# LayerNorm's scaling and split on ScalarE and VectorE, one cast for q and k, and another order for the first weights

## The chip, the cores and the metric

The kernel runs on one core of one Trainium2 chip. The metric is the time of one execution on the device, in microseconds (us); lower is better. The engines are named as the profile names them: PE (TensorE, matmuls and transposes), PEld (its weight loads), DVE (VectorE), ACT (ScalarE), POOL (GpSimd) and SP (SyncE, which issues the DMAs here). Each engine works through its own queue in the order in which the instructions were put there.

## What is computed

Eight batches, each with eight heads of block-causal attention over 576 positions, whose outputs are joined to 512 columns and go through a gated feed-forward part:

```python
# q, k, v: (8, 8, 576, 64); blocks of 64 positions
scores = (q @ k.T) / 8;  masked where block(i) < block(j)
attn   = softmax(scores)                   # sum + 1e-9 below
x      = attn @ v                          # joined over heads: (8, 576, 512)
h      = gelu(x @ w_in)                    # w_in: (512, 1024), tanh form
u, v   = h[..., :512], h[..., 512:]
v_n    = (v - mean(v)) / sqrt(var(v) + 1e-6) * g_ln
v_s    = w_sg @ v_n + b_sg                 # over positions, w_sg: (576, 576)
out    = x + (u * v_s) @ w_out             # w_out: (512, 512)
```

`w_in` and `w_out` arrive as float64 and are turned into float32 on the chip, from their words. Products with full precision are made of three products of a shorter float32 form: a value x is split into hi (x cast to that form) and lo (x minus hi), and hi*hi, hi*lo and lo*hi are added.

## The kernel before, in words

The unit of work is a pair of heads: 32 pairs (`PAIRS`), four for each batch. `slot(n, sc)` (line 724) does one pair: it finishes pair n (transposes of the probabilities, products with v, normalising) and makes the scores and exponents of pair n+1 in between. Four slots make a batch; with n counted from 0, the slots n % 4 = 0, 1, 2, 3 are called A, B, C and D here.

The feed-forward part of a batch is a generator in four parts that yield after every bank of results: `v_part` (5 pieces), `u_part` (8), `s_part` (8, the spatial product with w_sg) and `o_part` (8). After each D slot the parts of that batch are put on a list (line 821): v, u, the o of the batch before, then s. `hole(k)` (line 703) runs the next k pieces. Each slot has seven holes, and `PLAN` (line 720) says how many pieces each takes: all get one, the last of D two. `FIRST` (line 722) is the plan of the slots 4 to 7, in which there is no o yet: 21 pieces in 28 holes. So in the steady state A does v and two pieces of u, B six of u and one of o, C seven of o, and D eight of s.

Only PE keeps the order in which the program is written (`PIN`, line 58: `mm` and `turn` pin each matmul behind the instruction traced before it on PE). For DVE, ACT, POOL and SP the framework simulates the program with estimated durations and puts an instruction into the queue when its inputs and its buffer are there by that estimate; the written order is the priority among those that are ready. `paced` (line 522) pins a single instruction behind the one traced before it on its engine.

The LayerNorm of a batch is a list of small steps, `side`, that `run_side(k)` takes k at a time between the holes: GELU on ACT, `moments` (line 572, DVE), `inverse_std` (line 586, POOL), `centre` (line 579, DVE) and `scale` (line 590). `scale` handles one tile of 128 rows by 512: POOL multiplies by the inverse deviation in place, DVE casts the result to hi, POOL subtracts for lo. `s_part` begins by running all that is left of `side` (lines 645 to 647), and `need("s")` (line 644) runs the weight steps that are still missing.

Weights come in 30 steps (`weights`, line 274): 8 for v's half of w_in, 1 for the gains, 4 and 4 for u's half, 5 for w_sg, 8 for w_out. A step of w_in or w_out (`load_weight`, line 219) has a DMA of 256 KB, four parts ahead, one ACT and three DVE instructions that make float32 of float64 (`from_f64`, line 199; tiles `raw` and `w`), a cast on ACT and a subtraction on POOL. Four steps stand in the prologue (lines 805 to 813), and `load_share` (line 714) spreads `WS` (line 712) over the slots: 2, 2, 2, 2, 4, 3, 4, 4, 3.

`split_qk(n)` (line 125) casts q and k of a pair on DVE, one after the other, and subtracts on POOL; it stands in slot n-2. `va.split` (line 497) does the same for x, the attention's output; it is put off to the end of the next slot (`pending`, lines 774 to 793), except in D, where the one put off and D's own run at once. x is also stored to DRAM (`spill`), and `o_part` loads it again (tile `xr`, line 681) when it begins a column block, adds the result and stores it to `out_T` (line 697). x and xr share three buffers (`KINDS`, line 65). The inverse sums of the softmax are `inverse` (line 438).

Of the kernel before, what the change touches and what calls it, by code (L numbers as in the profile page):

```python
# [9 lines left out]
F32 = mybir.dt.float32  # L10
# [18 lines left out]
def kernel(  # L29
# [49 lines left out]
    def pbank(name):  # L79
        return bank("p", name, 3)  # L80

    def pin(ins, e):
        return tc.keep_in_program_order(ins) if e in PIN else ins

    def mm(*a, **k):
        return pin(nc.tensor.matmul(*a, **k), "P")  # L86
# [26 lines left out]
    def load_qk(n):  # L113
        b, h = PAIRS[n]
        if n == 0:

            q_f, k_f = page(F32, S, "w"), page(F32, S, "w")
        else:
            q_f = sp.tile([P, S], F32, tag="q_f", name="q_f", bufs=1)
            k_f = sp.tile([P, S], F32, tag="k_f", name="k_f", bufs=1)  # L120
        SP.dma_start(q_f, qT[b, h : h + 2].rearrange("a d s -> (a d) s"))
        SP.dma_start(k_f, kT[b, h : h + 2].rearrange("a d s -> (a d) s"))
        qk[n] = (q_f, k_f)

    def split_qk(n):
        q_f, k_f = qk[n]
        parts = []
        for x, name in ((q_f, "q"), (k_f, "k")):
            hi = sp.tile([P, S], F32R, tag=name + "_h", name=name + "_h")
            V.tensor_copy(hi, x)  # L130
            parts.append(hi)
        for x, name, hi in ((k_f, "k", parts[1]), (q_f, "q", parts[0])):
            lo = sp.tile([P, S], F32R, tag=name + "_l", name=name + "_l", bufs=1)
            G.tensor_tensor(lo, x, hi.bitcast(F32), op=ALU.subtract)
            parts.append(lo)
        q_h, k_h, k_l, q_l = parts
        qk[n] = [(q_h, k_h), (q_h, k_l), (q_l, k_h)]

    def load_v(n):
# [20 lines left out]
    mask = cp.tile([P, MW], BF16, name="mask")  # L160
    G.memset(mask, 0.0)
    G.memset(mask[:BLK, MW - BLK :], -8.0e9)
    half = cp.tile([P, NT], F32, name="half")
    G.memset(half, -0.5)
    stats = cp.tile([P, NT, 2], F32, name="stats")
# [33 lines left out]
    def from_f64(raw, dh, dl):  # L199

        n = raw.shape[-1]
        words = raw.bitcast(U32).rearrange("p (n t) -> p n t", t=2)
        hi, lo = words[:, :, 1], words[:, :, 0]
        tm = page(U32, 2 * n, "w")
        t, m = tm[:, :n], tm[:, n:]


        A.activation(m.bitcast(F32), hi.bitcast(F32), AF.Abs, scale=2.0**-112)

        V.tensor_scalar(t, lo, 29, None, op0=ALU.logical_shift_right)  # L210
# [79 lines left out]
    def need(part):  # L290

        while any(p == part for p, _ in weights):
            weight_step()
# [90 lines left out]
    class Values:  # L384
# [53 lines left out]
        def inverse(self):  # L438

            r = sp.tile([P, NT * 2], F32, tag="ri", name="ri", bufs=2)  # L440
            V.tensor_scalar_add(r, self.sm.rearrange("p i a -> p (i a)"), 1e-9)
            V.reciprocal(r, r)
            self.rx = sp.tile([P, NT, 2 * D], F32, tag="rx", name="rx", bufs=1)
            G.tensor_copy(
                self.rx.rearrange("p i (a d) -> p (i a) d", a=2),
                r.unsqueeze(2).broadcast_to([P, NT * 2, D]),
            )
# [63 lines left out]
    def run_side(k):  # L511

        while k > 0 and side and side[0][0] != "G":
            k -= 1
            side.popleft()[1]()
# [4 lines left out]
            side.popleft()[1]()  # L520

    def paced(ins, e):
        return ins if e in PIN else tc.keep_in_program_order(ins)

    def gelu(tiles, after):

# [8 lines left out]
    def accumulator(name):  # L535
        return sbank(name)

    def feed_forward(b):
# [4 lines left out]
        parts = (b, vv, vn, vn_t, u, g_s)  # L543
        return v_part(*parts), u_part(*parts), s_part(*parts), o_part(*parts)

    def v_part(b, vv, vn, vn_t, u, g_s):
        need("v")
        x_s = xs[b]
        for st in (NT - 1, *range(NT - 1)):
# [40 lines left out]
        def scale(st):  # L590
            x = vv[st]
            rows = x.shape[0]
            r = rs[:rows, st : st + 1]
            paced(G.tensor_tensor(x, x, r.broadcast_to([rows, DH]), op=ALU.mult), "G")
            if st < NT - 1:
                hi, lo = vn[st] = page(F32R, DH, "vh"), page(F32R, DH, "vl")
                V.tensor_copy(hi, x)
                G.tensor_tensor(lo, x, hi.bitcast(F32), op=ALU.subtract)
            else:
                V.tensor_copy(vone[:TAIL, :], x)  # L600
                V.tensor_copy(vn_t[:TAIL, :], x)
                V.tensor_tensor(
                    vn_t[BLK:, :], x, vn_t[:TAIL, :].bitcast(F32), op=ALU.subtract
                )

        side.append(("G", lambda: gelu(vv, last)))
        for st in range(NT):
# [4 lines left out]
        for st in (NT - 1, *range(NT - 1)):  # L612
            side.append(("V", lambda st=st: scale(st)))

    def u_part(b, vv, vn, vn_t, u, g_s):
        x_s = xs.pop(b)
        for fo in range(NC):
            need(f"u{fo}")
            u.append(page(F32, S, "u"))
            fs = slice(fo * P, (fo + 1) * P)  # L620
            for th in (0, 1):
# [18 lines left out]
                    side.append(("G", lambda: gelu(u, last)))  # L640
                yield "u"

    def s_part(b, vv, vn, vn_t, u, g_s):
        need("s")
        for _ in (0, 1):
            run_gelu()
            run_side(len(side))
        for dt in range(NC):
            ghi, glo = page(F32R, S, "gh"), page(F32R, S, "gl")
            g_s.append((ghi, glo))  # L650
            for th in (0, 1):
# [22 lines left out]
    def o_part(b, vv, vn, vn_t, u, g_s):  # L674
        need("o")
        x_r = {}
        for mo, th in [(mo, th) for mo in range(NC) for th in (0, 1)]:
            ts = slice(th * SH, (th + 1) * SH)
            if th == 0:
                x_r[mo] = page(F32, S, "xr")  # L680
                SP.dma_start(x_r[mo], spill.pop((b, mo)))
            x = x_r[mo]
            acc = accumulator("acco")
            ms = slice(mo * P, (mo + 1) * P)
# [24 lines left out]
            except StopIteration:  # L709
                work.popleft()  # L710

    WS = [2, 2, 2, 2, 4, 3, 4, 4, 3]

    def load_share(n, k):

# [3 lines left out]

    PLAN = ["1111111", "1111111", "1111111", "1111112"]  # L720

    FIRST = ["1111111", "1111111", "1010101", "1010010"]

    def slot(n, sc):
        va = Values(n, sc)
# [45 lines left out]
            nx.exponents(2)  # L771
        hole(g[4])
        va.normalise()
        last = n % (H // 2) == H // 2 - 1
        if last:
            for f in pending:
                f()
            pending.clear()
            va.split()
        run_side(2)  # L780
        if n + 2 < N:
            split_qk(n + 2)
# [3 lines left out]
        run_side(3)  # L786
        hole(g[6])
        run_side(3)
        for f in pending:
            f()  # L790
        pending.clear()
        if not last:
            pending.append(va.split)
        return nx

    pending = []
# [73 lines left out]
```

## Time and profile before

| | |
|---|---|
| median of 3 runs | 837.57 us (836.84 to 838.59) |
| the profiled execution | 838.82 us, its span 836.9 us |
| PE busy | 788.5 us, 94% of the span, 5926 instructions |
| DVE busy | 531.6 us, 64%, 1504 instructions |
| ACT busy | 424.4 us, 51%, 1124 instructions |
| POOL busy | 352.7 us, 42%, 402 instructions |
| HBM read and written | 45.78 MB and 18.87 MB |

The span goes from the first instruction to the end of the last one; the time of an execution holds some 2 us more. Rows of the profile name a line, an engine, an operation and its tiles as out<-in; line L99 and L86 are helpers through which nearly all instructions go, so tiles tell the groups apart. In a row of the timeline stand start, duration, engine, line, operation, tiles, shape and count, and in square brackets how long the engine had been idle and who ended that. PE's busy time counts matmuls whose ends are modelled, so a matmul that waits inside the pipeline can look busy. PEclk is the granted clock of TensorE as a share of full speed.

### The profile page before, as it was taken

The numbers are of one execution on the slowest core, as the hardware profiler recorded it, in microseconds if no ns is written. First come the engines' busy times: TensorE is split into PE (matmuls) and PEld (weight loads), VectorE is DVE, ScalarE is ACT, GpSimd is POOL, SyncE is SP. The second block draws the span as 40 slices with busy tenths as digits, with TensorE's granted clock in tenths as the row PEclk, the third lists the DMA queues.
The fourth block names the chain that finished last, engine by engine and source line by source line (L and its number), as shares of the span: only waits on it lengthen the run. The fifth ranks groups of instructions, "written<-read, shape, count | busy, mean of one in ns | idle before, by whom it ended". The sixth has DMA issues, their size and how long they took to land.

```text
span 836.9 us, 15898 instructions
## 1 busy us (share of the span) xinstructions
PE 788.5 (94%) x5926; PEld 649.0 (78%) x5926; DVE 531.6 (64%) x1504; ACT 424.4 (51%) x1124; POOL 352.7 (42%) x402
## 2 busy tenths in 40 slices
PE   5798992999999999999999999999999999999998
PEld 3466871878878888887887878788787878878998
DVE  6876474894865658564776747766586647753432
ACT  4776663656654367344653357642764446531400
POOL 5445158461543417432372513634164323713251
PEclk8799995999999999999999999999999999999999
DMA  7233205221122112310133101321123201230031
GB/s 251 77 114 115 85 18 159 80 61 57 44 86 99 58 58 72 126 59 30 58 108 120 58 28 31 126 101 57 58 71 122 77 16 57 75 112 29 1 114 71
DMA packets 46912, 65.67 MB, mean 78 GB/s; under 512 B 4082, under 2 KB 22514, under 8 KB 46836
## 3 DMA queue, kind: packets, MB, share of 16 engines
q1 hardware_dynamic: 46836, 64.67, 24.1%
q8 instruction: 46, 0.75, 0.4%
q14 instruction: 30, 0.25, 0.1%
HBM read 45.78 MB, written 18.87 MB: 77 GB/s over the span
## 4 chain that ended last, share of the span: by engine, by line
PE 63%; DVE 20%; ACT 6%; DMA 5%; POOL 3%; issue 3%; SPq 0%; DVEq 0%; ACTq 0%; POOLq 0%
PE accs L86 14%; PE accv L86 13%; PE acco L86 9%; PE ob L86 9%; PE s L86 7%; PE pb L89 3%; DVE prob L99 3%; DVE bs L99 3%; DVE vh L99 2%; DVE vv L99 2%; PE pa L89 2%; PE accu L86 2%; ACT prob L99 2%; PE pc L89 2%; DMA xr<-spill 2%
## 5 line engine op out<-in xcount | busy, mean ns | idle before, releaser
L99 ACT ACTIVATE prob<-prob,negm 128x448 f32<-128x448 f32 (+3 forms) x320 | 178.0, 558 | 157.8 <-DVE negm L99 154.1
L99 DVE CUSTOM_DVE_ANT_0 prob<-s,mask 128x288 f32<-128x288 f32 (+2 forms) x320 | 119.4, 421 | 37.2 <-PE s L86 36.5
L99 POOL TENSOR_TENSOR q_l<-q_f,q_h 128x576 fp32r<-128x576 f32 x31 | 44.2, 1425 | 196.1 <-PE s L86 158.3
L86 PE MATMUL ob<-pt,v_f 128*64 128x512 f32 (+4 forms) x640 | 115.3, 452 | 0.0
L99 POOL TENSOR_TENSOR gl<-u,gh 128x288 fp32r<-128x288 f32 x64 | 52.3, 824 | 105.1 <-DVE gh L99 72.9
L86 PE MATMUL accs<-ws_h,vh 128*128 128x288 f32 x256 | 79.8, 312 | 8.9 <-DVE vh L99 8.9
L86 PE MATMUL s<-k_h,q_h 64*128 64x288 f32 (+1 forms) x372 | 86.7, 351 | 1.2 <-DVE negm L99 1.2
L86 PE MATMUL accs<-ws_h,vl 128*128 128x288 f32 x256 | 76.8, 300 | 6.1 <-POOL vl L99 6.1
L86 PE MATMUL accu<-xh,wi_h 128*128 128x288 f32 x256 | 78.6, 307 | 1.3 <-ACT wi_h L99 1.3
L86 PE MATMUL acco<-gh,wo_h 128*128 128x288 f32 x256 | 79.8, 312 | 0.0
L86 PE MATMUL acco<-gl,wo_h 128*128 128x288 f32 x256 | 76.5, 299 | 0.0
L86 PE MATMUL acco<-gh,wo_l 128*128 128x288 f32 x256 | 76.4, 299 | 0.0
L86 PE MATMUL accs<-ws_l,vh 128*128 128x288 f32 x256 | 76.2, 298 | 0.0
L86 PE MATMUL accu<-xh,wi_l 128*128 128x288 f32 x256 | 75.4, 295 | 0.3 <-POOL wi_l L99 0.3
L86 PE MATMUL accu<-xl,wi_h 128*128 128x288 f32 x256 | 75.6, 295 | 0.0
L86 PE MATMUL s<-k_l,q_h 64*128 64x288 f32 (+1 forms) x372 | 72.2, 298 | 0.0
L86 PEld LDWEIGHTS ob<-pt,v_f 128*64 128x64 f32 x640 | 40.1, 139 | 40.9 <-issue 20.8
L86 PE MATMUL accv<-wi_h,xh 128*128 128x512 f32 x160 | 66.2, 414 | 0.7 <-POOL xh L99 0.7
L99 DVE TENSOR_TENSOR xr<-acco,xr 128x288 f32<-128x288 f32 x64 | 29.0, 454 | 59.2 <-PE acco L86 21.7
L86 PE MATMUL s<-k_h,q_l 64*128 64x288 f32 (+1 forms) x372 | 66.1, 293 | 0.0
L99 DVE TENSOR_TENSOR u<-accs,u 128x288 f32<-128x288 f32 x64 | 28.7, 448 | 57.6 <-PE accs L86 57.6
L86 PEld LDWEIGHTS s<-k_h,q_h 64*128 64x128 f32 x372 | 49.6, 180 | 18.2 <-issue 12.4
(106 smaller groups left out, 2109.9 us busy)
## 6 DMA issues: line engine op xcount, KB each, us to landing
spill<-x SPq DMA_DIRECT2D x32, 288.0 KB, 3.0
xr<-spill SPq DMA_DIRECT2D x32, 288.0 KB, 3.1
out_T<-xr SPq DMA_DIRECT2D x32, 288.0 KB, 2.4
q_f<-in_qT SPq DMA_DIRECT2D x31, 288.0 KB, 3.1
k_f<-in_kT SPq DMA_DIRECT2D x31, 288.0 KB, 3.4
v_f<-in_v SPq DMA_DIRECT2D x32, 256.0 KB, 3.3
raw<-in_w_in SPq DMA_DIRECT2D x16, 256.0 KB, 5.0
raw<-in_w_out SPq DMA_DIRECT2D x8, 256.0 KB, 4.3
```

The source lines that it names most:

```text
L86: return pin(nc.tensor.matmul(*a, **k), "P")
L89: return pin(nc.tensor.transpose(out, in_, identity), "P")
L99: return lambda *a, **k: pin(f(*a, **k), self.letter)
```

## The change

- **LayerNorm.** `scale` no longer uses POOL. ACT multiplies by the inverse deviation and casts in one instruction (hi), DVE makes lo = x*r - hi in one. For the 64-row tile ACT makes two such tiles, DVE one.
- **q and k.** Both lie in one tile, cast in one DVE instruction; POOL still subtracts in two, k first.
- **Weights.** Two steps instead of four in the prologue, at its end, and `WS` is 2, 2, 2, 1, 10, 3, 3, 3, 2: up to slot 3 that makes nine steps, v's eight and the gains; slot 4 has all of u's and two of w_sg's.
- **First pair.** DVE and ACT are pinned to the written order through the prologue (`kept`), in which `split_qk(1)` now stands behind all scores and exponents.
- **FIRST.** Still 21 pieces: 7, 6, 2, 6 instead of 7, 7, 4, 3, so s begins in the sixth hole of slot 6 instead of the last of slot 5.
- **x.** In A and B of the batches after the first the split is put off to the end of B; elsewhere it runs right after normalising.
- **xr.** The first block of o is loaded when u's last column block begins (for the last batch, at s's last), and each later one a block ahead.
- **Small ones.** The sum's 1e-9 is added by a two-tensor operation with a constant tile `tiny`; in `from_f64` a multiplication stands for an absolute value on ACT.

```diff
+    kept = set(PIN)
     def pin(ins, e):
-        return tc.keep_in_program_order(ins) if e in PIN else ins
+        return tc.keep_in_program_order(ins) if e in kept else ins
...
     def split_qk(n):
-        for x, name in ((q_f, "q"), (k_f, "k")):
-            hi = sp.tile([P, S], F32R, tag=name + "_h", name=name + "_h")
-            V.tensor_copy(hi, x)
-            parts.append(hi)
-        for x, name, hi in ((k_f, "k", parts[1]), (q_f, "q", parts[0])):
-            lo = sp.tile([P, S], F32R, tag=name + "_l", name=name + "_l", bufs=1)
-            G.tensor_tensor(lo, x, hi.bitcast(F32), op=ALU.subtract)
+        t = qk[n]
+        hi = sp.tile([P, 2, S], F32R, tag="qk_h", name="qk_h", bufs=1)
+        lo = sp.tile([P, 2, S], F32R, tag="qk_l", name="qk_l", bufs=1)
+        V.tensor_copy(hi, t)
+        for i in (1, 0):
+            G.tensor_tensor(lo[:, i, :], t[:, i, :], hi[:, i, :].bitcast(F32), op=ALU.subtract)
...
-        A.activation(m.bitcast(F32), hi.bitcast(F32), AF.Abs, scale=2.0**-112)
+        A.mul(m.bitcast(F32), hi.bitcast(F32), 2.0**-112)
...
-            V.tensor_scalar_add(r, self.sm.rearrange("p i a -> p (i a)"), 1e-9)
+            V.tensor_tensor(r, self.sm.rearrange("p i a -> p (i a)"), tiny, op=ALU.add)
...
         def scale(st):
-            paced(G.tensor_tensor(x, x, r.broadcast_to([rows, DH]), op=ALU.mult), "G")
             if st < NT - 1:
                 hi, lo = vn[st] = page(F32R, DH, "vh"), page(F32R, DH, "vl")
-                V.tensor_copy(hi, x)
-                G.tensor_tensor(lo, x, hi.bitcast(F32), op=ALU.subtract)
+                A.mul(hi, x, r)
             else:
-                V.tensor_copy(vone[:TAIL, :], x)
-                V.tensor_copy(vn_t[:TAIL, :], x)
-                V.tensor_tensor(
-                    vn_t[BLK:, :], x, vn_t[:TAIL, :].bitcast(F32), op=ALU.subtract
-                )
+                hi, lo = vn_t[:TAIL, :], vn_t[BLK:, :]
+                A.mul(hi, x, r)
+                A.mul(vone[:TAIL, :], x, r)
+            paced(V.scalar_tensor_tensor(
+                lo, x, r, hi.bitcast(F32), op0=ALU.mult, op1=ALU.subtract
+            ), "V")
...
     def u_part(...):
             need(f"u{fo}")
+            if fo == NC - 1 and b:
+                reloads[b - 1](0)
...
     def o_part(...):
+        if not x_r:
+            reload(0)
             if th == 0:
-                x_r[mo] = page(F32, S, "xr")
-                SP.dma_start(x_r[mo], spill.pop((b, mo)))
+                reload(mo + 1)
...
-    WS = [2, 2, 2, 2, 4, 3, 4, 4, 3]
+    WS = [2, 2, 2, 1, 10, 3, 3, 3, 2]
-    FIRST = ["1111111", "1111111", "1010101", "1010010"]
+    FIRST = ["1111111", "1111110", "0000011", "1111110"]
...
+        wait = n // (H // 2) > 0 and n % (H // 2) < 2
+        pending.append(va.split)
+        if not wait:
+            while pending:
+                pending.popleft()()
...
     load_v(0)
     load_qk(1)
+    kept.update("VA")
     sc = Scores(0)
     sc.step1()
     sc.exponents(1)
     sc.step2()
     sc.exponents(4)
-    weight_step()
     sc.step3()
     sc.exponents(3, 0)
-    split_qk(1)
-    weight_step()
     sc.step4()
     sc.exponents(2)
-    weight_step()
-    weight_step()
+    split_qk(1)
+    for _ in range(2):
+        weight_step()
+    kept.difference_update("VA")
```

More of the change, by code (lines that the diff above doesn't have):

```diff
@@ L118, in load_qk @@
         else:
-            q_f = sp.tile([P, S], F32, tag="q_f", name="q_f", bufs=1)
-            k_f = sp.tile([P, S], F32, tag="k_f", name="k_f", bufs=1)
+            t = sp.tile([P, 2, S], F32, tag="qk_f", name="qk_f", bufs=1)
+            q_f, k_f = t[:, 0, :], t[:, 1, :]
         SP.dma_start(q_f, qT[b, h : h + 2].rearrange("a d s -> (a d) s"))
         SP.dma_start(k_f, kT[b, h : h + 2].rearrange("a d s -> (a d) s"))
-        qk[n] = (q_f, k_f)
+        qk[n] = (q_f, k_f) if n == 0 else t
     def split_qk(n):
-        q_f, k_f = qk[n]
-        parts = []
-        for x, name in ((q_f, "q"), (k_f, "k")):
-            hi = sp.tile([P, S], F32R, tag=name + "_h", name=name + "_h")
-            V.tensor_copy(hi, x)
-            parts.append(hi)
-        for x, name, hi in ((k_f, "k", parts[1]), (q_f, "q", parts[0])):
-            lo = sp.tile([P, S], F32R, tag=name + "_l", name=name + "_l", bufs=1)
-            G.tensor_tensor(lo, x, hi.bitcast(F32), op=ALU.subtract)
-            parts.append(lo)
-        q_h, k_h, k_l, q_l = parts
+        t = qk[n]
[4 more added lines that the diff above has]
+            G.tensor_tensor(lo[:, i, :], t[:, i, :], hi[:, i, :].bitcast(F32), op=ALU.subtract)
+        q_h, k_h, q_l, k_l = hi[:, 0, :], hi[:, 1, :], lo[:, 0, :], lo[:, 1, :]
         qk[n] = [(q_h, k_h), (q_h, k_l), (q_l, k_h)]
@@ L162 @@
     G.memset(mask[:BLK, MW - BLK :], -8.0e9)
+    tiny = cp.tile([P, NT * 2], F32, name="tiny")
+    G.memset(tiny, 1e-9)
     half = cp.tile([P, NT], F32, name="half")
@@ L522, in paced @@
     def paced(ins, e):
-        return ins if e in PIN else tc.keep_in_program_order(ins)
+        return ins if e in kept else tc.keep_in_program_order(ins)
     def gelu(tiles, after):
@@ L536, in accumulator @@
         return sbank(name)
+    reloads = {}
     def feed_forward(b):
@@ L542, in feed_forward, with reload, v_part @@
         vn_t = sp.tile([P, DH], F32R, tag="vn_t", name="vn_t")
-        parts = (b, vv, vn, vn_t, u, g_s)
+        x_r = {}
+        def reload(mo):
+            if mo < NC:
+                x_r[mo] = page(F32, S, "xr")
+                SP.dma_start(x_r[mo], spill.pop((b, mo)))
+        parts = (b, vv, vn, vn_t, u, g_s, x_r, reload)
         return v_part(*parts), u_part(*parts), s_part(*parts), o_part(*parts)
-    def v_part(b, vv, vn, vn_t, u, g_s):
+    def v_part(b, vv, vn, vn_t, u, g_s, x_r, reload):
         need("v")
@@ L613, in v_part, with u_part @@
             side.append(("V", lambda st=st: scale(st)))
-    def u_part(b, vv, vn, vn_t, u, g_s):
+    def u_part(b, vv, vn, vn_t, u, g_s, x_r, reload):
         x_s = xs.pop(b)
@@ L641, in u_part, with s_part @@
                 yield "u"
-    def s_part(b, vv, vn, vn_t, u, g_s):
+    def s_part(b, vv, vn, vn_t, u, g_s, x_r, reload):
         need("s")
@@ L647, in s_part @@
             run_side(len(side))
+        reloads[b] = reload
         for dt in range(NC):
+            if dt == NC - 1 and b == B - 1:
+                reload(0)
             ghi, glo = page(F32R, S, "gh"), page(F32R, S, "gl")
@@ L672, in s_part, with o_part @@
                 yield "s"
-    def o_part(b, vv, vn, vn_t, u, g_s):
+    def o_part(b, vv, vn, vn_t, u, g_s, x_r, reload):
         need("o")
-        x_r = {}
+        if not x_r:
+            reload(0)
         for mo, th in [(mo, th) for mo in range(NC) for th in (0, 1)]:
@@ L773, in slot @@
         va.normalise()
[L774 to L779, printed above, removed]
+        wait = n // (H // 2) > 0 and n % (H // 2) < 2
[3 more added lines that the diff above has]
+                pending.popleft()()
         run_side(2)
@@ L788, in slot @@
         run_side(3)
[L789 to L793, printed above, removed]
+        if n % (H // 2) == 1:
+            while pending:
+                pending.popleft()()
         return nx
-    pending = []
+    pending = deque()
     last_o = []
```

## The prediction

> **What bounds the kernel now.** I first read the page's strips, then cut the span at the first transpose of each slot and asked for busy time in these windows.
>
> ```profile
> PEclk8799995999999999999999999999999999999999
> ```
> ```profile
> 0.00:16.80 16.80, 10.13 (x42) 6.62 (x42) 9.27 (x25) 6.47 (x16) 8.39 (x37) 0.88 0.83 280
> 16.80:41.50 24.70, 15.64 (x96) 9.21 (x96) 22.49 (x78) 19.18 (x61) 12.46 (x16) 0.67 0.27 87
> 52.20:63.60 11.40, 10.29 (x97) 6.92 (x95) 8.84 (x34) 8.47 (x29) 5.29 (x7) 1.00 0.32 104
> 102.90:146.30 43.40, 26.86 (x184) 21.13 (x183) 26.93 (x63) 23.32 (x55) 29.12 (x27) 0.76 0.30 94
> 146.30:165.20 18.90, 18.90 (x153) 16.01 (x152) 16.27 (x49) 13.17 (x36) 7.51 (x8) 0.92 0.20 58
> 165.20:180.70 15.50, 15.50 (x138) 12.61 (x137) 15.28 (x48) 9.73 (x31) 10.28 (x14) 1.00 0.17 55
> 230.30:256.30 26.00, 24.47 (x181) 19.77 (x180) 17.00 (x45) 12.61 (x33) 13.95 (x16) 0.93 0.37 117
> 505.00:526.90 21.90, 21.70 (x181) 18.43 (x180) 19.37 (x52) 15.07 (x41) 10.69 (x10) 1.00 0.13 41
> 526.90:550.80 23.90, 22.99 (x182) 18.81 (x181) 17.11 (x45) 12.68 (x33) 14.00 (x16) 1.00 0.39 124
> 720.80:745.10 24.30, 22.89 (x181) 18.75 (x180) 15.22 (x43) 12.70 (x33) 11.20 (x12) 1.00 0.26 86
> ```
>
> Each row: stretch, length, busy time of PE, PEld, DVE, ACT and POOL, granted clock, DMA share, GB/s. The rows are the prologue, slots 0, 2, 5, 6, 7, then C slot 10, B slot 21, C slot 22 and C slot 30. A slot with attention alone takes 11.4 us with 10.29 us of PE. PE's price of the feed-forward parts stands in the chain that ended last, where they run alone at the end:
>
> ```profile
> 780.34 12.74 PE accu L86 x96
> 793.08 12.72 PE acco L86 x96
> 805.80 14.84 PE accs L86 x112
> ```
>
> A B slot (three quarters of u, 9.56, an eighth of o, 1.59, attention 10.3) needs 21.4 us of PE and takes 21.9: PE is the bound. Three places are above that. Slot 0 takes 24.7 us. Slots 5 to 7 take 43.4 + 18.9 + 15.5 = 77.8 us, for 9.56 of u, 14.84 of s and three attentions, 55.3 us. A C slot needs 11.13 of o and 10.3, 21.4 us, and takes 23.9 to 26.0. Any gain comes from these.
>
> **The start.** The DVE and ACT timelines, and windows of the instructions on tiles `w` (DVE: weight conversion) and `prob` (one slot's scores and exponents):
>
> ```profile
> 9.51 1.32 DVE L99 TENSOR_SCALAR w<-raw 128x256 uint32<-128x256 uint32 x1 [0.31 <-DMA raw<-in_w_in]
> ...
> 12.28 0.45 DVE L99 CUSTOM_DVE_ANT_0 prob<-s,mask 128x288 f32<-128x288 f32 x1
> ```
> ```profile
> 25.04 0.18 ACT L99 ACTIVATION_READ_ACCUMULATOR prob<-prob,negm 128x1 f32 x1
> ```
> ```profile
> 6.00:25.10 19.10, 6.03 (x24) 2.75 (x24) 11.68 (x31) 7.17 (x19) 5.73 (x8) 0.68 0.77 255
> ```
> ```profile
> 52.20:63.60 11.40, 3.97 (x30) 2.72 (x30) 4.69 (x12) 6.06 (x22) 0.00 (x0) 1.00 0.32 104
> ```
>
> The first maximum stands behind weight work, at 12.28, and the last exponent ends at 25.2. Pinned, maxima come first. They could start about 5 us earlier, near 7 (an estimate: the q and k casts and weight rows ahead of 12.28 fall away); 6.06 us of exponents, starved in part by DVE, end near 14.5. The prologue then gives 25.2 - 14.5 = 10.7 us. But DVE's 11.68 us of weight work (31 instructions, ten steps) is moved, not removed. An attention slot leaves DVE 11.4 - 8.84 = 2.6 us idle. Hidden in the four slots, 10.4 us, it costs 1.3 of the 10.7; crowded into slots 0 and 1, 5.2 us, it costs 6.5. The plan also puts three steps less ahead of slot 4 (nine against twelve), 3.5 us at 1.17 a step. I take 7 us gained, between 4.2 and 9.4 and near the middle; the range keeps 0 (the planner fills all weights in early again) and 10.7.
>
> The prologue's q/k split now waits behind the scores; its cast and two POOL subtractions end before pair 1's scores are due after slot 0's transposes, so it costs nothing; if late, slot 0 starts 2 us later.
>
> **Slots 4 to 7.** PE's own waits, the SP queue and DVE:
>
> ```profile
> 113.39 0.40 PE L86 MATMUL accu<-xh,wi_h 128*128 128x288 f32 x1 [1.29 <-ACT wi_h L99]
> ...
> 133.86 0.61 PE L86 MATMUL accs<-ws_h,vl 128*128 128x288 f32 x1 [4.65 <-POOL vl L99]
> 140.49 0.58 PE L86 MATMUL accs<-ws_h,vh 128*128 128x288 f32 x1 [5.78 <-DVE vh L99]
> ```
> ```profile
> 131.34 0.61 SPq L99 DMA_DIRECT2D w<-in_b_sg x2
> ```
> ```profile
> 136.07 2.06 DVE L99 TENSOR_TENSOR ws_l<-w,ws_l 1x576 fp32r<-1x576 f32 x1 [7.42 <-ACT ws_l L99]
> ```
>
> s begins in slot 5's last hole, where neither v's normalised tiles nor w_sg's last parts are there: b_sg is only issued at 131.34, DVE sits idle for 7.42 us with casts of vh behind it, and PE follows; the clock falls to 0.76 over the slot. In the new plan w_sg's steps end in slot 5 and `side` empties in slot 5, while s begins five holes into slot 6: at 10.3 us per slot's attention there is about half a slot, 6 us or more, between the last of them and the first matmul of s. The stall goes with its cold clock. What is late next is PE's own work: 9.56 + 14.84 + 3 x 10.3 = 55.3, and slot 6, with five empty holes, has the attention slot's 1.1 us of gaps, 56.4. A wait like the 1.29 us on u's weights may stay, since slot 4 now converts eight such parts: 57.8. Gain 77.8 - 57.8 = 20 us, bounds 12 (half the stall comes back) to 21.4. For slots 4 and 8 I book nothing.
>
> **The C slots.** Slot 26 in DVE's and SP's timelines:
>
> ```profile
> 621.65 1.65 DVE L99 CAST vh<-vv 128x512 fp32r<-128x512 f32 x1
> 623.22 1.39 DVE L99 TENSOR_SCALAR ri<-sums 128x10 f32<-128x10 f32 x1
> ...
> 635.25 0.46 DVE L99 TENSOR_TENSOR xr<-acco,xr 128x288 f32<-128x288 f32 x1 [3.71 <-DMA xr<-spill]
> ```
> ```profile
> 632.38 0.80 SPq L99 DMA_DIRECT2D xr<-spill x2
> ```
>
> DVE enters C late with LayerNorm's casts, then stands 3.71 us before an addition whose xr was issued only at 632.38; behind it in DVE's queue stand the copies of transposes for which PE waits. Now xr is asked for a block ahead, x's buffers come free at B's end, and the casts are gone from DVE's queue. The six C slots take 26.0, 25.7, 25.5, 23.9, 23.8 and 24.3 (the first and the fourth and the last are shown), 149.2 in all; at 21.4 each they need 128.4. Of the 20.8 I take two thirds, 14: DVE's xh casts and its copies of PE's banks still meet there. Bounds 3 to 20.8.
>
> **The clock in C.** C slots 10 and 22 hold the same work and idle alike, yet one has a clock of 0.93 and takes 2.1 us more. Should C keep its stall in part, three of six slots may or may not lose that again; this is 6 us inside the range. TensorE: Matmul & The Clock Gate in the Trainium skill (What's actually happening) lays such a drop to a free-running window of about 3.4 us; by it, a mere shift of the start could cool all six C slots, 6 us more, or none.
>
> **LayerNorm itself.** Groups:
>
> ```profile
> L99 POOL TENSOR_TENSOR vv<-vv,rs 128x512 f32<-128x512 f32 (+1 forms) x40 | 43.8, 1101 | 5.0 <-DVE vv L99 5.0
> L99 POOL TENSOR_TENSOR vl<-vv,vh 128x512 fp32r<-128x512 f32 x32 | 42.2, 1320 | 19.5 <-DVE vh L99 19.5
> ```
> ```profile
> L99 DVE CAST k_h<-k_f 128x576 fp32r<-128x576 f32 x31 | 34.6, 1115 | 0.3 <-DMA k_f<-in_kT 0.3
> ...
> L99 DVE CAST vh<-vv 128x512 fp32r<-128x512 f32 x32 | 29.1, 909 | 12.3 <-POOL vv L99 12.1
> ...
> L99 DVE SCALAR_TENSOR_TENSOR vv<-vv,stats,g_bc 128x512 f32<-128x512 f32 (+1 forms) x40 | 28.2, 740 | 0.0
> ```
> ```profile
> L99 ACT COPY vv<-accv 128x512 f32<-128x512 f32 x32 | 18.8, 587 | 51.6 <-PE accv L86 51.6
> ```
>
> POOL loses 86.0 us in all, 10.8 a batch. A batch adds six multiplications on ACT at about 0.6 (the copy's 587 ns), 3.5 us, in B, where ACT has 21.9 - 15.07 = 6.8 us free, and five 0.74 us operations on DVE against four casts of 0.91 and the tail's. All lies beside PE. The new wait is ACT's: a multiplication waits for POOL's inverse deviation, with exponents queued behind it; DVE's lo, pinned, waits for ACT with maxima behind it. With cover gone each would cost one such wait, under 1 us a batch; I book 0. The q/k cast: two of at most 1.1 us become one, between 0.9 less and 0.5 more, beside PE except in slots 0 to 3; the added constant costs one small fill; the multiplication for the absolute value costs the same. All 0.
>
> **Sum.** 836.9 - 7 - 20 - 14 = 795.9 of span. The profiled execution took 838.8, 1.9 above its span: 797.8, say 798. That execution is 1.2 above the median of the runs, inside their spread.
>
> **Rivals.**
> (1) The planner packs the weights into slots 0 and 1 whatever the plan says: the order of a queue is the simulation's, not the written one. For it: slot 0's 22.49 us of DVE in 24.7. Against: fewer steps and pinned scores. The start gains 0 to 2: 804.
> (2) C keeps its stall, because DVE and not the buffer is behind. Casts of 512 elements take 0.91 on average but 1.65 with POOL at work, and the row at 136.07 took 2.06 us for 576 elements with two inputs, against 0.74 for 512 elsewhere: POOL holds up two-input operations too, so the new lo and the new `ri` would wait as the casts did. C then gains 4: 808. Advanced Engine Details and Errata in the Trainium skill (GPSIMD Details) says that POOL shares a read and a write interface with DVE, in conflict with two-port modes and with two SBUF inputs; it speaks against the two-input forms, and the 2.06 us agrees.
> (3) Slot 4's ten steps crowd DVE and ACT, LayerNorm comes late, s still waits: 12 of 20 gained: 806.
> (4) Slower than before: the third x buffer. In B, x of A is now held to B's end while the first xr already holds a second one, and B's x takes the third. If each of B and C must then wait for an output store before normalising, PE's banks stay full for a wait like the 3.71 us. Twice in seven batches that is 52 us, without C's 14 gained: 798 + 14 + 52 = 864. Slower than before from (838 - 812) / 14 = 1.9 us a slot on. Against it: A's x is released before C needs a buffer, and the load asks early without anything on PE waiting for it.
>
> **How the numbers follow.** Forecast 0.55, (1) 0.17, (2) 0.14, (3) 0.09, (4) 0.05. A measurement of this kernel cannot tell less than about 0.2% from no change. Forecast and rivals 1 to 3 are all faster, 0.95; from that I take 0.02 for several falling short at once, which goes to no change, 0.02. Faster 0.93, same 0.02, slower 0.05. The range: below, start and s at their best and C in full, 798 - 3.7 - 1.4 - 6.8 = 786; above, (1) with most of (2), 814.
>
> **What would show it.** Right: no PE wait on vl or vh above 1 us around the first s; slots 5 to 7 under 60 us; the last prologue exponent before 16 us and slot 4's start before 70; C slots near 22.5 with xr issued a block ahead; POOL below 270 us. Wrong: a new wait of ACT for rs or of x for a buffer, weight work again dense on DVE before 35 us, or C still at 24.

## The result and the profile after

The changed kernel takes 805.11 us (median of 4 runs, 802.79 to 805.46) against 837.21 of the kernel before in the same measurement: a ratio of 0.9618, 95% interval 0.9581 to 0.9656. The forecast of 798 us, 786 to 814, holds it. Its sum does not: one of its three terms has the wrong sign, and the largest gain has another source. These are windows of the kernel after, cut at the first transpose of each slot (columns as in the windows of before): prologue, slots 0, 1 and 2, slots 5, 6 and 7, C slot 10, B slot 21.

```profile
0.00:9.50 9.50, 7.69 (x43) 5.68 (x43) 2.81 (x15) 3.21 (x8) 3.38 (x33) 1.00 0.76 238
9.50:33.90 24.40, 16.98 (x96) 10.58 (x96) 23.02 (x74) 18.58 (x55) 13.74 (x15) 0.72 0.57 191
33.90:55.90 22.00, 14.06 (x97) 8.67 (x96) 13.40 (x49) 13.52 (x42) 16.55 (x17) 0.77 0.28 92
55.90:69.40 13.50, 11.99 (x98) 7.65 (x97) 8.48 (x32) 8.59 (x29) 5.33 (x6) 0.87 0.27 88
...
111.10:130.80 19.70, 19.70 (x169) 16.65 (x167) 16.68 (x47) 17.54 (x45) 5.51 (x6) 1.00 0.20 65
130.80:151.30 20.50, 16.80 (x126) 11.98 (x125) 18.96 (x53) 18.12 (x47) 14.45 (x16) 0.83 0.46 147
151.30:172.60 21.30, 21.30 (x182) 18.25 (x180) 18.20 (x52) 10.66 (x32) 12.05 (x15) 1.00 0.19 62
220.70:242.00 21.30, 21.30 (x181) 18.26 (x180) 12.70 (x42) 12.80 (x33) 8.65 (x11) 1.00 0.48 144
480.90:502.20 21.30, 21.30 (x181) 18.25 (x181) 17.75 (x51) 18.52 (x47) 5.21 (x6) 1.00 0.08 27
```

Slot by slot, from the same cuts in both traces:

| stretch | before | after | difference | forecast |
|---|---|---|---|---|
| prologue | 16.8 | 9.5 | -7.3 | |
| slots 0 to 3 | 58.3 | 73.4 | +15.1 | |
| both together | 75.1 | 82.9 | +7.8 | -7 |
| slots 5 to 7 | 77.8 | 61.5 | -16.3 | -20 |
| the six C slots | 149.2 | 127.9 | -21.3 | -14 |
| the six B slots | 131.5 | 127.9 | -3.6 | 0 |
| slots 4 and 8 | 55.5 | 55.0 | -0.4 | 0 |
| all else | 347.8 | 347.9 | 0 | 0 |
| span | 836.9 | 803.1 | -33.8 | -41 |

From slot 9 on PE has no idle time in a B or C slot: its busy time is the whole window, at a clock of 1.00. The kernel is bound by PE there. From PE's waits in the kernel after (total, times, longest):

```profile
PE pa L91 <- ACT prob L101: 8.7, 7, 4.6
...
PE ob L88 <- ACT pt L101: 2.5, 1, 2.5
```

The waits on vh and vl are gone, as forecast; the longest for probabilities, 4.6 us, lies in slot 1. The start in DVE's and ACT's timelines, then the windows of slots 0 and 1 for DVE's instructions on tile `w`, the weight conversion:

```profile
6.69 0.46 DVE L101 CUSTOM_DVE_ANT_0 prob<-s,mask 128x288 f32<-128x288 f32 x1 [6.69 <-PE s L88]
```
```profile
13.06 0.19 ACT L101 ACTIVATION_READ_ACCUMULATOR prob<-prob,negm 128x1 f32 x1
```
```profile
9.50:33.90 24.40, 15.89 (x43) 0.72 0.57 191
33.90:55.90 22.00, 2.28 (x6) 0.77 0.28 92
```

The first maximum starts at 6.69 instead of 12.28, and the prologue's last exponent ends at 13.2 instead of 25.2. But 18.2 us of DVE's weight work follow in slots 0 and 1, 15.9 of it in slot 0. All 16 conversions of `w_in` (the instructions `w<-raw` with one input) run in slot 0, none ahead of it; the written plan has eight of them up to slot 3. Before, five ran in the prologue and ten in slot 0. And slot 1 takes 22 us, with PE busy for 14 of them.

The new operations, in the groups of after (busy, mean ns):

```profile
L101 ACT ACTIVATE vh<-vv,rs 128x512 fp32r<-128x512 f32 x32 | 23.3, 727 | 2.3 <-POOL rs L101 2.3
```
```profile
L101 DVE TENSOR_TENSOR ri<-sums,tiny 128x10 f32<-128x10 f32 x32 | 26.2, 817 | 19.9 <-ACT prob L101 18.6 <-POOL qk_l L101 1.3
L101 DVE SCALAR_TENSOR_TENSOR vl<-vv,rs,vh 128x512 fp32r<-128x512 f32 x32 | 25.6, 816 | 1.2 <-ACT vh L101 1.1
...
L101 DVE CAST xh<-x 128x576 fp32r<-128x576 f32 x32 | 20.6, 658 | 0.6
```

DVE's timeline of after at the entry of C slot 26, which answers to the rows of before at 621.65 to 635.25:

```profile
593.91 0.64 DVE L101 TENSOR_TENSOR x<-pe,x 128x512 f32<-128x512 f32 x1
...
595.60 1.34 DVE L101 CAST xh<-x 128x576 fp32r<-128x576 f32 x2
...
599.73 0.46 DVE L101 CUSTOM_DVE_ANT_0 prob<-s,mask 128x288 f32<-128x288 f32 x1 [0.44 <-PE s L88]
```

And the same entry before:

```profile
620.85 0.69 DVE L99 TENSOR_TENSOR x<-pe,x 128x512 f32<-128x512 f32 x1
...
624.78 2.59 DVE L99 CAST xh<-x 128x576 fp32r<-128x576 f32 x2
...
630.16 0.44 DVE L99 CUSTOM_DVE_ANT_0 prob<-s,mask 128x288 f32<-128x288 f32 x1
```

From the start of x's large multiplication (the first row of each) to the next pair's first maximum it was 9.3 us, with two casts of vh and the `ri` of 1.39 us in between; now it is 5.8, and at its end it is DVE that waits for PE (0.44 us).

### The profile page after: what moved, and what is told of

Its sections match the earlier page's. It is cut to its first block, busy times and chain, and to the rows that moved or that the text cites. A ratio compares the mean times of both kernels' runs of the same rounds, so it can differ in the third digit from the quotient of the medians.

```text
span 803.1 us, 15777 instructions
## 1 busy us (share of the span) xinstructions
PE 774.1 (96%) x5926; PEld 642.1 (80%) x5926; DVE 488.6 (61%) x1457; ACT 452.4 (56%) x1172; POOL 273.9 (34%) x331
## 4 chain that ended last, share of the span: by engine, by line
PE 83%; ACT 0%; DVE 0%; issue 0%
PE accs L88 15%; PE acco L88 13%; PE accv L88 12%; PE accu L88 11%; PE ob L88 10%; PE s L88 9%; PE pb L91 4%; PE pc L91 3%; PE pa L91 3%; PE pe L91 1%; PE pd L91 1%; PE pd L88 0%; ACT pt L101 0%; DVE xr L101 0%; ACT w L101 0%
## 5 line engine op out<-in xcount | busy, mean ns | idle before, releaser
L101 ACT ACTIVATE prob<-prob,negm 128x448 f32<-128x448 f32 (+4 forms) x320 | 177.5, 557 | 107.3 <-DVE negm L101 104.6
L101 POOL TENSOR_TENSOR qk_l<-qk_f,qk_h 128x576 fp32r<-128x576 f32 x62 | 89.3, 1461 | 270.3 <-PE pe L91 114.0
L101 DVE CUSTOM_DVE_ANT_0 prob<-s,mask 128x288 f32<-128x288 f32 (+2 forms) x320 | 119.2, 422 | 78.9 <-PE s L88 77.4
L88 PE MATMUL ob<-pt,v_f 128*64 128x512 f32 (+4 forms) x640 | 111.7, 455 | 2.5 <-ACT pt L101 2.5
L88 PE MATMUL s<-qk_h 64*128 64x288 f32 (+1 forms) x372 | 83.2, 353 | 0.0
L88 PE MATMUL s<-qk_l,qk_h 64*128 64x288 f32 (+1 forms) x372 | 70.1, 297 | 0.9 <-POOL qk_l L101 0.9
L88 PE MATMUL s<-qk_h,qk_l 64*128 64x288 f32 (+1 forms) x372 | 65.5, 297 | 1.9 <-POOL qk_l L101 1.9
L88 PE MATMUL accv<-wi_l,xh 128*128 128x512 f32 x160 | 63.0, 393 | 0.0
```

Of the source, the lines that this page charges most:

```text
L101: return lambda *a, **k: pin(f(*a, **k), self.letter)
```

## The experiments

Theory T, formed on these traces: the gain of the C and B slots and most of that of slots 5 to 7 comes from LayerNorm's scaling leaving POOL and DVE's queue; the start loses because the planner moves u's weights into slot 0. Rivals: the earlier loads of xr and the x buffers (the forecast's reading of C), the split of x, and the new order of the first pair. For each run stand its edit, what was expected, and what came out; ratios are to the kernel before.

**LayerNorm alone, in the kernel before.**

```diff
-            paced(G.tensor_tensor(x, x, r.broadcast_to([rows, DH]), op=ALU.mult), "G")
...
-                V.tensor_copy(hi, x)
-                G.tensor_tensor(lo, x, hi.bitcast(F32), op=ALU.subtract)
+                A.mul(hi, x, r)
...
+            paced(V.scalar_tensor_tensor(
+                lo, x, r, hi.bitcast(F32), op0=ALU.mult, op1=ALU.subtract
+            ), "V")
```

> The kernel before, with LayerNorm's new scaling and split alone (ACT multiplies and casts, DVE makes lo). Theory now (LayerNorm's work on POOL and DVE was the main hold-up of the C slots, of B's small idle time and of the first s): C falls from 23.8 to 26.0 down to 22 or less, B from 21.9 to 21.3, and the stall of slots 5 to 7 shrinks by 5 to 10 us; the time falls by 20 to 32 us. Rival (the earlier split of x is what frees C): C stays at 23 or more, the time falls by less than 12 us.

Measured: 807.87 us, 0.9637 (0.9612 to 0.9661). The interval overlaps that of the whole change: this one function alone gives as much as the whole. That does not make the other parts idle: they gain a further 6.8 us in slots 5 to 7 (68.3 here, 61.5 in after) and lose 5.5 by the start of slot 4 (77.4 here, 82.9 in after). Slots 5 to 7 and C slot 22 of this run:

```profile
105.20:138.20 33.00, 24.12 (x184) 19.48 (x183) 25.00 (x60) 26.18 (x60) 18.17 (x17) 0.92 0.34 105
138.20:158.00 19.80, 19.80 (x153) 16.80 (x152) 17.33 (x51) 13.40 (x37) 8.34 (x9) 0.87 0.26 84
158.00:173.50 15.50, 15.50 (x138) 12.61 (x137) 15.19 (x48) 9.14 (x28) 9.39 (x13) 1.00 0.16 51
...
504.70:526.00 21.30, 21.30 (x181) 18.25 (x180) 13.74 (x42) 12.81 (x33) 9.17 (x11) 1.00 0.41 132
```

C is at 21.3, and slots 5 to 7 fall from 77.8 to 68.3. Slot 4 starts 2.3 us later than before (75.1), although LayerNorm has no work ahead of it; what moved it, no run shows. The waits on vh and vl are gone; what is late next is w_sg, in PE's waits in slot 5:

```profile
PE accs L86 <- ACT ws_h L99: 4.0, 1, 4.0
PE accs L86 <- POOL ws_l L99: 2.1, 2, 1.8
```

**LayerNorm back on POOL and DVE, the rest as after.**

```diff
-                A.mul(hi, x, r)
+                V.tensor_copy(hi, x)
+                G.tensor_tensor(lo, x, hi.bitcast(F32), op=ALU.subtract)
```

(and the multiplication on POOL ahead of it and the tail's casts, as before; DVE's one-instruction lo is gone)

> The changed kernel, with LayerNorm's scaling and split as before: the multiplication and lo on POOL, the casts on DVE. The buffer theory: C stays at 21.3, the time rises by at most 5 us. The rival (LayerNorm's work on DVE and POOL is what held up C): C returns to 23 or more and the time rises by 12 to 20 us. If both are needed, either run alone loses most of C's gain.

Measured: 820.81 us, 0.9806 (0.9778 to 0.9834), 16 us above after. Slot 6, B slot 21 and C slot 22:

```profile
131.50:159.50 28.00, 20.25 (x125) 13.70 (x124) 22.17 (x52) 16.66 (x42) 23.02 (x24) 0.82 0.44 149
494.00:515.90 21.90, 21.71 (x181) 18.43 (x180) 19.49 (x53) 15.09 (x41) 10.71 (x10) 1.00 0.09 29
515.90:538.20 22.30, 22.15 (x182) 18.78 (x181) 15.71 (x42) 12.67 (x33) 13.66 (x16) 1.00 0.38 126
```

The time rises as the rival had it, but C, at 22.1 to 22.8, does not reach its 23. Slot 6 loses 7.5 us, each B 0.6, each C 1.0. In the kernel before a C slot lost 3.5 (149.2 over six is 24.9, against 21.3). So with LayerNorm on POOL some other part of the change takes 2.5 us off a C slot, a part that is worth nothing once LayerNorm has left. Which one it is was not separated.

**POOL's work without the chain.** After, with 72 operations on POOL that nobody waits for, the same number and size as LayerNorm had there; the gains change by rounding.

```diff
+            g, t = g_bc[:rows, :], tiny[:rows, 0:1].broadcast_to([rows, DH])
+            paced(G.tensor_tensor(g, g, t, op=ALU.add), "G")
+            if st < NT - 1:
+                G.tensor_tensor(g, g, t, op=ALU.subtract)
```

> After, with GpSimd given back the work that LayerNorm's scaling took from it, but off every chain: beside each of the five scalings it adds 1e-9 to the gains g_bc in place, and for four of the five takes it away again (128x512, two inputs, the second a broadcast column), 72 operations of 1.1 to 1.4 us, some 90 us of GpSimd in all, as many as the multiplications and subtractions that it had in before. The gains are changed by rounding alone. Theory P (the gain came from GpSimd's time: its queue and the VectorE operations that stand while it works): the C slots rise from 21.31 to 22.5 or more, the two-input VectorE operations get longer again, median 812 to 822. Rival Q (the gain came from the shorter chain from the statistics to vh and vl, so that work on GpSimd which nobody waits for is free): C slots within 0.4 us of 21.31, median 803 to 808.

Measured: 816.19 us, 0.9753 (0.9721 to 0.9785), 11 us above after. C slot 22, three groups of DVE, and DVE's and POOL's timelines at the entry of C slot 26:

```profile
508.90:531.80 22.90, 22.41 (x182) 18.49 (x181) 16.32 (x43) 13.03 (x33) 12.96 (x15) 1.00 0.43 135
```
```profile
L101 DVE SCALAR_TENSOR_TENSOR vl<-vv,rs,vh 128x512 fp32r<-128x512 f32 x32 | 40.6, 1287 | 0.0
...
L101 DVE TENSOR_TENSOR ri<-sums,tiny 128x10 f32<-128x10 f32 x32 | 34.5, 1077 | 13.4 <-ACT prob L101 12.1 <-POOL qk_l L101 1.3
L101 DVE CAST xh<-x 128x576 fp32r<-128x576 f32 x32 | 30.5, 968 | 0.6
```
```profile
602.62 0.64 DVE L101 TENSOR_TENSOR x<-pe,x 128x512 f32<-128x512 f32 x1
...
604.29 2.89 DVE L101 CAST xh<-x 128x576 fp32r<-128x576 f32 x2
...
609.57 0.44 DVE L101 CUSTOM_DVE_ANT_0 prob<-s,mask 128x288 f32<-128x288 f32 x1
```
```profile
602.39 3.26 POOL L101 TENSOR_TENSOR qk_l<-qk_f,qk_h 128x576 fp32r<-128x576 f32 x2
605.61 1.25 POOL L101 TENSOR_TENSOR g_bc<-g_bc,tiny 128x512 f32<-128x512 f32 x1
```

Work on POOL that DVE, ACT and PE never wait for costs 11 us, 9.3 of it in the six C slots (1.5 each). The same DVE operations are longer: vl 1.29 instead of 0.82 us, xh 0.97 instead of 0.66. The two casts of x take 2.89 us with two-input operations on POOL beside them (the second `qk_l` and `g_bc`), and end 0.3 us after `g_bc` does; in after the pair takes 1.34. The way to the first maximum is 6.95 us instead of 5.8, and the pair alone is longer than that difference. Whether PE is held by DVE's standing only, or also by POOL's own queue (xl and the others come later too), these rows do not part. The rival, that only the chain to vh and vl was too long, is out for C. It stands for slot 6, which is 21.7 here and 28.0 with the chain back on POOL, and for the B slots, which stay at 21.3 here and take 21.9 there. The added work is a stand-in, not LayerNorm's own: in C it costs even more than LayerNorm on POOL did in the run above (1.5 against 1.0).

**xr loaded as before, the rest as after.** In `o_part` each block is loaded when it begins; the early load in `u_part` is gone.

```diff
-            if fo == NC - 1 and b:
-                reloads[b - 1](0)
...
-                reload(mo + 1)
+                reload(mo)
```

> The changed kernel, with xr loaded as before: at the beginning of its own column block, none ahead. The buffer theory of the forecast (C slots stalled because xr came late): C slots go back from 21.3 us to about 23.8, six of them, and the time rises by 12 to 20 us. The rival (C was late because LayerNorm's casts and POOL's work stood in front on DVE; that is gone in either case): C stays under 22 us and the time rises by less than 4 us.

Measured: 804.30 us, 0.9609 (0.9583 to 0.9634), as after. C slot 22:

```profile
501.10:522.40 21.30, 21.30 (x181) 18.25 (x180) 12.74 (x42) 12.85 (x33) 8.64 (x11) 1.00 0.42 131
```

**The split of x alone, in the kernel before** (the `pending` lines of the diff, nothing else).

> The kernel before, with the new place of x's split alone. Theory now: C stays above 23 us, the time changes by less than 5 us. Rival (the earlier split frees x's buffers and with them C): C falls to 22.5 or less, the time falls by 8 us or more. Loading xr ahead has already moved nothing when it was taken back.

Measured: 836.83 us, 0.9999 (0.9979 to 1.002); C slots 23.8 to 25.8. With LayerNorm moved, C's gain needs neither the early loads nor the split; the early loads alone in the kernel before were not run. What DVE waited for behind xr tells the same: the group of before, and that of LayerNorm alone, which loads xr as before.

```profile
L99 DVE TENSOR_TENSOR xr<-acco,xr 128x288 f32<-128x288 f32 x64 | 29.0, 454 | 59.2 <-PE acco L86 21.7 <-DMA xr<-spill 20.4 <-issue 13.3
```
```profile
L99 DVE TENSOR_TENSOR xr<-acco,xr 128x288 f32<-128x288 f32 x64 | 29.2, 456 | 52.2 <-PE acco L86 40.6 <-issue 8.6 <-DMA xr<-spill 2.4
```

With the load unchanged, the wait for it falls from 20.4 to 2.4 us. With LayerNorm back on POOL it is still 11.7 us, although xr is loaded ahead in that run.

**q and k in two casts, the rest as after** (`split_qk` and its tiles as in the removed lines of the diff).

> The changed kernel, with q and k in tiles of their own and cast in two instructions, as before. Slots 2 and 3 hold attention alone and take 13.5 us after the change, 11.4 before. If the one cast, which stands behind the last maxima and holds up POOL's subtractions, is the cause: both return to about 11.4 and the time falls by 3 to 6 us. If the cause is another (the order of ACT's copies and exponents, the earlier split of x): no change within 2 us.

Measured: 804.04 us, 0.9602 (0.9574 to 0.9630): no difference in the whole, where 3 to 6 us less had been expected if the one cast is the cause. Slots 2 and 3 do take 11.5 instead of 13.5 us, but slots 5 and 8 are longer. Nor is the cast shown to be what held slots 2 and 3: the run with xr loaded as before has the one cast and takes 11.9 in each.

**Every weight step after the prologue in the written order**, on DVE and ACT.

```diff
     def weight_step():
+        kept.update("VA")
         while weights and next(weights[0][1], None) is None:
             weights.popleft()
+        kept.difference_update("VA" if not prologue else "")
```

> The changed kernel, with the weight steps' DVE and ACT instructions pinned to the written order in all slots, so that by the queue 1, 3, 2, 2, 0, 8 conversions stand in the prologue and slots 0 to 4 where 1, 14, 0, 0, 0, 0 stood. Planner theory (slots 0 and 1 take 24.5 and 22.0 us because DVE's queue holds fourteen conversions there): both fall to 13 to 16 us, slot 4 grows by at most 3, the time falls by 10 to 16 us. Rival (the same work is in the way wherever it is put): what slots 0 and 1 gain comes back in slots 2 to 4, the time changes by less than 4 us.

Measured: 800.88 us, 0.9565 (0.9541 to 0.9588), 4 us below after. Conversions that run in slots 0 to 4: 4, 2, 2, 0, 8 (16, 0, 0, 0, 0 in after), the forecast's picture of the plan. Slot 4 starts at 73.6, nine us sooner than in after; slots 5 and 7 give back 5.7. Slots 0 to 3, and PE's largest wait in the run:

```profile
9.80:73.60 63.80, 51.94 (x382) 33.70 (x381) 49.45 (x162) 41.72 (x132) 26.83 (x31) 0.81 0.34 110
```
```profile
PE pa L91 <- DVE x L101: 9.9, 4, 2.8
```

DVE has 12.4 us of weight work here, 2.3 to 4.0 a slot, and is idle for 14; yet the four slots take 63.8 us, 18 more than four of attention alone (11.4). In the written order `ri` and weight instructions stand ahead of x in DVE's queue, and PE waits for x: 7.3 of the 9.9 us lie in these slots. ACT, kept in order too, stands 7.9 us there before casts whose weights DVE has not made, and PE waits 4.5 us for its probabilities. How the 18 us divide between the two engines was not separated.

**Prologue and `WS` of before, the rest as after.**

> The changed kernel, with the prologue and the weights' plan of before (four steps in the prologue, DVE and ACT unpinned there, WS as before), and the new plan of the first s. Theory now (the pinned prologue ends ten us earlier, but u's and w_sg's conversions are packed into slots 0 and 1 and take more than that back): slot 4 starts near 75 us instead of 82.9, and the time falls by 3 to 8 us. Rival (slots 0 and 1 suffer from something else in the change): slot 4 starts at 80 or later, no change within 2 us. The weights of w_sg come later here, so slots 5 and 6 may give back 2 to 4 us.

Measured: 803.83 us, 0.9608 (0.9587 to 0.9629), as after. Five conversions run ahead of slot 0, ten in slot 0; slot 4 starts at 78.7, slots 5 to 7 take 64.1. The start is 4 us better, and the later weights cost 3: the time is the rival's (no change), and slot 4's start lies between the 75 and the 80 that the two had expected.

**The later weights in the written order, v's free**, with q and k in two casts.

```diff
+        if weights and weights[0][0] != "v" and not prologue:
+            kept.update("VA")
```

> The changed kernel, with the weight steps of u, w_sg and w_out pinned to the written order on DVE and ACT, v's free for the planner, and q and k cast in two. The queue holds 1, 7, 0, 0, 0, 7 conversions in the prologue and slots 0 to 4. Planner theory: slots 0 and 1 lose about seven conversions, 8 to 9 us, slots 2 and 3 are attention slots of 11.5, slot 4 grows by 1 or 2: 795 to 799 us, better than the version with all steps pinned (800.9). Rival (what is moved comes back in slots 4 to 7): 800 to 804 us.

Measured: 799.03 us, 0.9540 (0.9525 to 0.9555). That is just above the 795 to 799 that the theory expected. Slot 4 starts at 70.3; slot 5 takes 24.6, with a wait of PE of 3.3 us for ACT's copy of probabilities.

**Only u's weights in the written order**, with q and k in two casts.

```diff
+        pinned = "VA" if weights and weights[0][0][0] == "u" else ""
+        kept.update(pinned)
```

> After with q and k in two tiles and two casts (as before) and with the order of VectorE and ScalarE kept as written only while a step of u's weights is issued; the steps of v, s and the output's weights stay free for the planner. Conversions of the weights in VectorE's queue: 1 ahead of slot 0, 7 in slot 0, 7 in slot 5, 4, 2 and 2 in slots 7 to 9. Theory (the weight work that the planner crowds into slot 0 costs some 10 us at the start, and what the run with all late weights written in order gave back in slots 5 and 8 came from ScalarE standing behind casts whose data had not landed): slot 4 starts at 70 to 72 us (82.9 in after, 70.3 with all late weights written in order), slot 5 takes 21 to 23 (24.63 there), slot 8 26 to 27 (28.0 there), median 794 to 798. Rival (u's own seven conversions in slot 5 cost it, whoever issues the rest): slot 5 24 or more and slots 5 to 7 67 or more, median 798.5 to 801.

Measured: 795.42 us (794.48 to 797.50), 0.9510 (0.9485 to 0.9535): faster than both kernels, about 9 us below after. Slots 0 and 1, then slots 5, 6 and 7:

```profile
10.00:35.00 25.00, 16.62 (x95) 10.35 (x96) 22.38 (x70) 17.16 (x54) 13.03 (x15) 0.73 0.42 135
35.00:47.10 12.10, 10.40 (x97) 7.19 (x96) 9.76 (x34) 8.03 (x27) 4.84 (x7) 1.00 0.32 100
```
```profile
98.20:121.80 23.60, 21.35 (x169) 18.22 (x168) 18.85 (x47) 21.06 (x50) 10.27 (x10) 0.93 0.22 69
121.80:141.50 19.70, 16.73 (x125) 12.11 (x124) 19.46 (x53) 17.57 (x45) 13.56 (x14) 0.83 0.55 181
141.50:162.80 21.30, 21.30 (x182) 18.26 (x181) 17.29 (x55) 10.69 (x32) 12.72 (x16) 1.00 0.21 67
```

With nine conversions in slot 0 and seven in slot 4, slot 1 falls from 22 to 12.1 us and slot 4 starts at 70.4 instead of 82.9. The run with two casts alone has slot 1 at 22.2, so it is the weights. Slot 0 keeps its 25 us, and slots 5 to 7 give back 3: both the theory and its rival had expected other sizes there, slot 5 below 23 or slots 5 to 7 above 67; they take 23.6 and 64.6. Slot 8 takes 27.4, where 26 to 27 had been expected.

**The same, with pieces put into slot 6's empty holes.**

```diff
-    FIRST = ["1111111", "1111110", "0000011", "1111110"]
+    FIRST = ["1111111", "1111000", "1000100", "1111112"]
```

> As the run with only u's steps kept as written, and the first pair of slots 5 to 7 takes other pieces: FIRST = 1111111, 1111000, 1000100, 1111112 instead of 1111111, 1111110, 0000011, 1111110. Slot 6 of after has five empty holes and 20.47 us with a PE busy of 16.76, so pieces put there should cost little of its own, and be missing elsewhere. Theory (slots 5 to 7 are held by where the pieces stand against the attention's own waits): slot 5 loses two pieces and falls by 1.5 to 3 us, slot 6 stays within 1 us, slots 5 to 7 together 3 to 5 us less than in the run without this, median 791 to 795. Rival (u, the GELU behind it and s are in one chain, and a piece that is moved later only moves its wait): slots 5 to 7 within 1.5 us of that run or longer, median within 2 us of it or above.

Measured: 798.01 us, 0.9539 (0.9515 to 0.9563), 2.6 above the run without it. Slots 5 and 7 (slot 6 takes 20.1):

```profile
98.40:120.30 21.90, 18.12 (x146) 14.21 (x145) 16.36 (x41) 19.38 (x42) 9.29 (x8) 0.92 0.38 121
...
140.40:167.40 27.00, 25.30 (x209) 22.05 (x207) 25.19 (x59) 16.71 (x43) 18.61 (x22) 1.00 0.29 86
```

Slot 5 gives up a third of its u, with 3.2 us of PE's busy time, and falls by 1.7 only; slot 7 pays 5.7 for the pieces of s that it takes over. The sizes are the rival's; the chain that it gives as the reason was not traced.

**`FIRST` as before, the rest as after** (the diff's line, turned round).

> After with the written order of the first pair as before (FIRST = 1111111, 1111111, 1010101, 1010010); all else as in after. Before spent 77.8 us in slots 5 to 7, before with LayerNorm's change alone 68.3, after 61.5. Theory A (the new order of pieces is what made the last 6.8 us, by giving u the time in which s waits on the GELU): slots 5 to 7 take 66 to 69 us with a wait of s or of the s operand in slot 5, median 809 to 812. Theory B (the earlier weights did it: all conversions of u's weights are done by 39.5 us in after, as in before by 34.7, so this is not likely): slots 5 to 7 stay at 61 to 63, median 804 to 806.

Measured: 804.55 us, 0.9613 (0.9585 to 0.9640), as after: slots 5 to 7 take 26.9, 19.0 and 15.5, 61.4 in all against 61.5. PE's wait for s is there, smaller than before:

```profile
PE accs L88 <- DVE vl L101: 3.7, 2, 2.6
```

So of the 16.3 us that slots 5 to 7 gained, LayerNorm alone gave 9.5; the other parts without `FIRST` gave 6.9, with the waits for w_sg's tiles of the run with LayerNorm alone gone; the new order gave nothing on top.

## Why the prediction was right and wrong

**The total** was right by luck, since its parts were not: the start came 14.8 us worse than booked and slots 5 to 7 3.7 worse, C 7.3 and B 3.6 better, which leaves the 7 us by which the span misses its 795.9. Of the signs that it named, the waits on vl and vh are gone and the last prologue exponent comes before 16; slots 5 to 7 (61.5, not under 60), slot 4's start (82.9, not before 70) and POOL (273.9 us, not below 270) missed, and one sign of being wrong came true, weight work dense on DVE before 35 us.

**The start failed** at the step "DVE's 11.68 us of weight work (31 instructions, ten steps) is moved, not removed ... Hidden in the four slots, 10.4 us, it costs 1.3". Its first half held: the last prologue exponent ends at 13.2 (forecast 14.5), slot 0 starts 7.3 us sooner, where 10.7 was booked. The second half is refuted twice. The work isn't spread, since all 16 conversions run in slot 0: rival 1, whose mechanism came true, but whose gain of 0 to 2 was a loss of 7.8. And where the run with every step in order does spread it, in DVE time that is idle by the windows, the four slots still lose 18 us. Idle time of DVE was not free room there: what the written order put ahead of x held PE for 7.3 of these 18 us, by PE's waits. And not all of the 7.8 is the plan's: with prologue and plan of before slot 4 still starts at 78.7, and with LayerNorm alone at 77.4.

**Slots 5 to 7** were right in sign and in what goes: no wait on vh or vl above 1 us. The gain is 16.3 where 20 was booked. The forecast gave it to w_sg's steps, `side` and the later s together; shown is that LayerNorm's change alone carried 9.5 and the order of s nothing. What is late next was not PE's own work alone: slot 6, at a PE busy of 16.8 in 20.5, waits for ACT's copies (ob, 2.5 us) and has a clock of 0.83.

**The C slots** were mis-sized, 21.3 for 14, and in part wrongly explained: "Now xr is asked for a block ahead, x's buffers come free at B's end, and the casts are gone from DVE's queue". That the casts leave DVE's queue was right; the rest plays no part once LayerNorm has moved, since C stays at 21.30 with xr loaded as before, and LayerNorm's change alone takes DVE's waits on xr from 20.4 to 2.4 us. That wait came with LayerNorm's place; whether it had a share of its own in the loss before was not separated.

**LayerNorm at 0** was the step that hid the result: "All lies beside PE". That held for the added operations, which cost PE nothing in the B and C slots (21.3 us, all of it PE's busy time) although they came out longer than booked (ACT 0.73 for 0.6, DVE's lo 0.82 for 0.74). It did not hold for those that were removed. Their 86 us on POOL cost PE, by the run with as much POOL work that nobody waits for, 11 us, with DVE operations that take longer while POOL works. Rival 2 had this mechanism, on the row of 2.06 us, and used it only against the change: the new `ri` does still stand at 0.82 us for ten elements a row, as does the old one-input form in the run with LayerNorm alone (0.81). But with 79 us less on POOL there was less to stand for. Advanced Engine Details and Errata in the Trainium skill (GPSIMD Details) names an interface shared by POOL and DVE, in conflict with two SBUF inputs; that run's rows for vl and `ri` agree (1.29 and 1.08 us, against 0.82 for both in after). What they show belonged on the gain's side as well.

**The clock.** Whether the C slots would be cooled was left open. They were not: PE has no idle time there and the clock is 1.00; slots 2 and 3 have 0.87 instead (next but one section). The two C rows that the forecast called idle alike are not quite so: 1.5 us in slot 10, 0.9 in slot 22. The rule of a free-running window (TensorE: Matmul & The Clock Gate in the Trainium skill, What's actually happening) is neither borne out nor ruled out by these runs.

**Rivals 3 and 4**: s does not wait, and no wait for an x buffer shows among PE's waits in after.

**Open**: which other part takes 2.5 us off a C slot while LayerNorm is on POOL; and why slot 0 takes 23 to 25 us with 9, 10 or 16 conversions in it alike, but 16.5 with four.

## What to carry to other kernels

Before an operation on a side engine is priced at zero, ask whom it slows by working: here 88 us of POOL on no chain cost 11 us of the kernel, seen as longer means of DVE's two-input operations and casts. A plan written as steps per slot says little where a scheduler orders the queue; count the instructions in the queue between two fixed marks, and pin the ones that must be late. And price each part of a change alone: here one function alone gave as much as the whole, and holding back the steps of one weight gave some 8 us beyond the run with two casts alone (0.9510 against 0.9602).

## What the runs showed of the hardware that was not expected

Two plain casts of 576 elements a row took 1.34 us with one copy on POOL beside them and 2.59 to 2.89 us with two-input operations there. POOL's timeline beside the pair in after (595.60 to 596.94):

```profile
595.11 1.15 POOL L101 COPY rx<-ri 128x640 f32<-128x640 f32 x1
```

Taken one by one, 60 of the 96 casts of x in before, in after and in the run with POOL's extra work take over 0.6 us (14, 18 and 28 of 32). Each of the 60 began while a POOL operation was running, and ended 0.31 to 0.36 us after a POOL operation did; the other 36 took 0.45 to 0.59. So in these traces a long cast looks like a short one that stood until POOL's operation was through, not like one that ran slower throughout.

And the same attention slot, with the same work on every engine, takes 13.5 us at a clock of 0.87 in after (the row at 55.90) and 11.9 at 1.00 in the run with xr loaded as before:

```profile
57.90:69.80 11.90, 10.57 (x97) 7.19 (x96) 8.61 (x32) 8.35 (x27) 5.34 (x6) 1.00 0.30 100
```

Neither run has weight work there, and DVE, ACT and POOL are busy alike. The slot starts 2 us later in the second; what gave it the other clock, no run shows.
